# A planner that knows how TensorE's array is divided: biases planned head by head, and times nearer to the trace

## The chip, the cores and the metric

The kernel runs on one core of a Trainium2 chip. The metric is the device time of the whole kernel in microseconds; of the kernel before it is 848.01 us, the median of three runs (847.74 to 849.63). One more execution was profiled: it took 847.26 us, and the rows below are from it.

A core has five engines that run side by side, each through its own list of instructions in order: TensorE (PE, matrix products; PEld is its loading of weights), VectorE (DVE), ScalarE (ACT), GpSimd (POOL) and SyncE (SP, which here issues DMA transfers). They wait for each other by semaphores.

## What is computed

A windowed attention with a few global keys, then two feed-forward networks (FFN), each on the output of the one before. Cut to what matters:

```python
# attention: batch 2, 8 heads, 768 positions, 64 per head
scores = q @ k.T / sqrt(64) - slope[head] * dist       # kept: 96 positions back, 8 global keys
a = exp(scores - max); a = a / (a.sum() + 1e-9)
x = (a @ v) as 1536 tokens x 512

# first FFN: 4 experts, all applied, weighted by p of the token; 512 -> 1024 -> 512
out = sum over e of p[:, e] * (relu(x @ w1[e]) @ w2[e])

# second FFN: 512 -> 2048 -> 512; w_in and w_out arrive as 64-bit floats
h = out @ w_in;  g = h * clip(h + 3, 0, 6) / 6;  return g @ w_out
```

## The kernel before

**Attention.** The work is 24 pairs of a chunk of 256 queries and two heads. For a pair TensorE makes the scores (L351: products with 64 rows, the two heads in the two halves of the array's rows), VectorE adds the bias and takes the smallest value (L366), ScalarE the exponential (L381), VectorE the sums (L392, L393), POOL normalises (L401), TensorE transposes (L420, the whole array), ScalarE and VectorE copy the result out (L437, L442), and TensorE multiplies by the values (L457: 64 columns, the two heads in the two halves of the array's columns).

**FFNs.** Both run as 48 steps: 0 to 31 for the four experts of the two batches, 32 to 39 for the second FFN of batch 0 and 40 to 47 of batch 1. A step forms the first product of two blocks of 128 hidden columns by seven smaller products (m1 to m7, six matmuls of 384 columns each: a high and a low part stand for one fp32 number, L909, L913, L916). m1, m6, m7 and m4 add up in one PSUM bank ("x"), between them ScalarE takes snapshots of it (L933); m2, m5 and m3 go through another bank ("w"), and VectorE adds a snapshot to each of them (L946): m2 makes the corner c11, m5 c22, m3 c12. The bank is free for the next product when the corner is read. The corners become the hidden parts hh and hl (second FFN: L1000, L1003, L1017, L1023), and the second product "O" uses them in 48 matmuls of 512 or 256 columns a step (L1088, L1091, L1092). Weights come in as "wr" (L775), go through ScalarE (the high part, L250) and VectorE (the low part, L255), for steps of batch 0 also through sums (L832).

**Conversions.** The second FFN's weights are 64-bit floats. Beside the steps of the first FFN, 32 conversions turn half a step's weights each into fp32: a load (L691), seven VectorE instructions (L701, L707, L713, L720, L725, L731, L743), and a store to DRAM (L747). Conversions 30 and 31 are the last: the load of step 39's w1 (L775) waits for conversions 28 and 30, that of its w2 for 29 and 31.

**What sets the order.** A planner (class Plan) is given each piece of work with an engine, a cost in us, what it comes after, and a rank. `emit` simulates the engines by these costs: the engine that is free first takes the ready piece of the lowest rank, and the instructions are written out in that order, which each engine then keeps. A piece on another engine is ready LATENCY (0.25 us) after the one that it waits for, after a load 2.0. Where the simulation shows TensorE idle in the attention, small filler matmuls are put in (L263). So the table of costs decides the order on all engines at once. The ranks: a conversion has 100000 and more, behind all else, so it gets VectorE when nothing else is ready. The functions that the diff touches, and what calls them:

Of the kernel before, what the change touches and what calls it, by code (L numbers as in the profile page):

```python
# [17 lines left out]
ALU = mybir.AluOpType  # L18
# [3 lines left out]
P = 128  # L22
# [13 lines left out]
WIN = FAR + P  # L36
# [9 lines left out]
FIRST_LOAD = 1.0  # L46
HUGE = 3.0e38
NEG = -1.0e9
T_SCORES, T_TURN, T_VALUES = (0.95, 1.2), (0.8, 1.05), (0.75, 0.97)
NONE = -4.0e12  # L50
SLOPES = [2.0 ** (-8.0 * (h + 1) / H) for h in range(H)]

# [6 lines left out]
class Plan:  # L59
# [5 lines left out]


    LOAD = 2.0
    LATENCY = 0.25

    def __init__(self, idle=None):  # L70
        self.pieces = []
        self.ported = set()
        self.idle = idle

    def add(self, engine, cost, emit, after=(), rank=0.0, port=False):

        self.pieces.append((engine, cost, emit, after, rank))
        if port or engine == "pool":
            self.ported.add(len(self.pieces) - 1)
        return len(self.pieces) - 1  # L80
# [9 lines left out]
    def emit(self):  # L90
        n = len(self.pieces)
        missing, ready, followers = [0] * n, [0.0] * n, [[] for _ in range(n)]
        free, later, now, ended = {}, {}, {}, {}
        port = 0.0
        for i, (engine, _, _, after, _) in enumerate(self.pieces):
            after = set(self.flat(after))
            missing[i] = len(after)
            for a in after:
                followers[a].append(i)
            free.setdefault(engine, 0.0)  # L100
            later.setdefault(engine, [])
            now.setdefault(engine, [])
        for i in range(n):
            if not missing[i]:
                heappush(later[self.pieces[i][0]], (0.0, i))
        count = 0
        while count < n:
            best = None
            for engine in free:
                while later[engine] and later[engine][0][0] <= free[engine]:  # L110
                    i = heappop(later[engine])[1]
                    insort(now[engine], (self.pieces[i][4], i))

                for place, (rank, i) in enumerate(now[engine]):
                    if i not in self.ported or port <= free[engine]:
                        start = free[engine]
                        break
                else:
                    events = [port] * bool(now[engine]) + [t for t, _ in later[engine][:1]]
                    place, start = None, min(events, default=None)  # L120
                if start is not None and (best is None or start < best[0]):
                    best = (start, engine, place)
            start, engine, place = best
            if place is None:
                free[engine] = start
                continue
            i = now[engine].pop(place)[1]
            count += 1
            _, cost, emit, _, _ = self.pieces[i]
            if i in self.ported:  # L130
                port = start + cost
            if self.idle:
                self.idle(engine, start - ended.get(engine, 0.0))
            emit()
            free[engine] = ended[engine] = start + cost
            for j in followers[i]:
                other = self.pieces[j][0]
                lag = 0.0 if other == engine else self.LOAD if engine == "load" else self.LATENCY
                ready[j] = max(ready[j], start + cost + lag)
                missing[j] -= 1  # L140
                if not missing[j]:
                    heappush(later[other], (ready[j], j))
# [3 lines left out]
def moe_attention_kernel(ctx, tc, qk, vw, sizes, dpt, w1, w2, w_in, w_out, ident_d, fast_d, slow_d, out):  # L146
    nc = tc.nc
# [22 lines left out]
    base = const.tile([P, P + WIN], F32, name="base")  # L170
# [7 lines left out]
    with tc.manual_schedule(engines={mybir.EngineType.DVE}):  # L178
# [3 lines left out]
            out=nv[:, 0:2], in0=nv[:, 2:4], scalar=4294967296.0, in1=lo, op0=ALU.mult, op1=ALU.add  # L182
# [38 lines left out]
    def pools(bx, fast):  # L221
# [43 lines left out]
        plan = Plan(keep_warm)  # L265
# [8 lines left out]
        started = {}  # L274
# [37 lines left out]
        def plan_pair(i, c, hp, tabs, place_users, normalised, biased, outs, x_bank):  # L312
# [40 lines left out]
                            raw[rows, w0 : w0 + WIN][:, used[qb]], start=True, stop=True,  # L353
                        )

            s_in = plan.add("pe", T_SCORES[kinds[0]], scores, [loaded] + waits, rank)
            readers.append(s_in)
            weighed = []
            for qb in range(CH):

                def bias(qb=qb, kind=kinds[qb], used=used[qb]):
                    if "t" not in m:
                        m["t"] = att.tile([P, CH, 2, WIN], F32, tag="t", name=f"t_{u}", bufs=3)
                        m["mn"] = att.tile([P, CH, 2], F32, tag="mn", name=f"mn_{u}", bufs=4)
                    for j in range(2):
                        nc.vector.tensor_tensor_reduce(  # L366
                            out=m["t"][:, qb, j, used], in0=m["s", j][:, qb * WIN : (qb + 1) * WIN][:, used],
                            in1=(base if hp == j == 0 else tabs[:, 2 * hp + j - 1])[:, kind * P : P + kind * WIN],
                            scale=-0.125, scalar=HUGE, op0=ALU.add, op1=ALU.min, accum_out=m["mn"][:, qb, j : j + 1],
                        )  # L370

                after = [s_in, started[2 * hp, kinds[qb]], started[2 * hp + 1, kinds[qb]]]
                e = plan.add("dve", 0.72 if kinds[qb] else 0.5, bias, after + wait_t, rank)
                for su in s_users:
                    su.append(e)
                biased[i].append(e)

                def exponentials(j, qb=qb, used=used[qb]):
                    if "sm" not in m:
                        m["sm"] = att.tile([P, CH, 2], F32, tag="sm", name=f"sm_{u}", bufs=4)  # L380
                    nc.scalar.activation(  # L381
                        m["t"][:, qb, j, used], m["t"][:, qb, j, used], AF.Exp, bias=m["mn"][:, qb, j : j + 1],
                        scale=-1.0, accum_out=m["sm"][:, qb, j : j + 1],
                    )

                for j in range(2):
                    weighed.append(
                        plan.add("act", 0.48 if kinds[qb] else 0.39, lambda j=j, f=exponentials: f(j), [e], rank)
                    )

            def sums():
                nc.vector.tensor_scalar(out=m["sm"][:], in0=m["sm"][:], scalar1=1e-9, scalar2=None, op0=ALU.add)  # L392
                nc.vector.reciprocal(m["sm"][:], m["sm"][:])  # L393

            r = plan.add("dve", 0.4, sums, weighed, rank)
            normal = []
            for qb in range(CH):
                for j in range(2):
# [4 lines left out]
                            scalar2=1.0, op0=ALU.mult, op1=ALU.mult,  # L403
                        )

                    normal.append(plan.add("pool", 0.46 if kinds[qb] else 0.32, normalise, [r], rank))
            normalised[i] += normal
            wait_a, a_users = [], []
            for qb in range(CH):
# [4 lines left out]
            def turn(qb):  # L414
# [7 lines left out]
                            )  # L422

            turns = [
                plan.add("pe", 0.57 if kinds[qb] else 0.3, lambda qb=qb: turn(qb), normal[2*qb:2*qb+2] + wait_a[qb:qb+1], rank)
                for qb in range(CH)
            ]
            t_users += turns
# [30 lines left out]
                                m["at", qb][:n, j, h, :], start=h == 1 - kinds[qb], stop=h == 1,  # L459
                            )  # L460

            v = plan.add("pe", T_VALUES[kinds[0]], values, [e for e, _ in copied] + [v_in, biased[i + 2] if b else outs[i - 2]], rank)
            v_users.append(v)
            for _, at_users in copied:
                at_users.append(v)
# [807 lines left out]
```

## Time and profile before

| | us |
|---|---|
| median of three runs | 848.01 |
| profiled execution | 847.26 |
| its span | 845.2 |
| TensorE busy | 833.7 |
| VectorE busy | 655.2 |
| ScalarE busy | 402.0 |
| POOL busy | 68.1 (all in the attention) |

The span goes from the first instruction to the last; 2.06 us of the execution lie around it. "Busy" counts the time in which an engine works at an instruction; matmuls overlap, so a busy TensorE shows that work is there and not how fast it goes. A wait is listed with the instruction that waited and what ended it last. Starts are counted from the span's start. A row of the timeline gives the start and the busy time; of matmuls the busy time reaches into the next one's, so the time of a matmul among others is read from start to start.

### The profile page before, as it was taken

What the parts mean: (1) busy time and instruction counts of PE and PEld (TensorE: products, weight loads), DVE (VectorE), ACT (ScalarE), POOL (GpSimd) and SP (SyncE); (2) the same over time, 40 slices, a digit from 0 to 9 for tenths busy, and PEclk for the clock granted to TensorE, in tenths of its full rate; (3) what the DMA queues carried; (4) which work ended last, traced back from release to release, by engine and by line L of the source; (5) the groups of instructions that cost most, each with busy time, mean ns of one, the idle gap of its engine ahead of it and who ended that gap; (6) DMA issues with size and microseconds to landing.
All of it is one profiled execution on the core that took longest, in us unless ns stands there. A gap on an engine that the chain in (4) does not pass through costs nothing.

```text
span 845.2 us, 13646 instructions
## 1 busy us (share of the span) xinstructions
PE 833.7 (99%) x5090; PEld 763.2 (90%) x5090; DVE 655.2 (78%) x1366; ACT 402.0 (48%) x850; POOL 68.1 (8%) x131
## 2 busy tenths in 40 slices
PE   8999999999999999999999999999999999999997
PEld 6777999999999999999999999999999999999996
DVE  6999989988998977987777688689898766545442
ACT  6998643543433433543333333335666455545441
POOL 5888200000000000000000000000000000000000
PEclk9999999999999999999999999999999999999999
DMA  7873454465565565645656664744452555534302
GB/s 264 314 221 94 175 202 153 138 211 181 166 209 194 165 222 180 204 150 179 216 172 199 208 208 158 234 165 140 174 163 103 172 186 185 190 125 139 136 1 79
DMA packets 56985, 147.34 MB, mean 174 GB/s; under 512 B 6480, under 2 KB 7760, under 8 KB 56912
## 3 DMA queue, kind: packets, MB, share of 16 engines
q1 hardware_dynamic: 56480, 145.69, 52.2%
q8 instruction: 42, 0.69, 0.3%
q10 hardware_dynamic: 432, 0.71, 0.3%
q14 instruction: 31, 0.25, 0.1%
HBM read 109.66 MB, written 36.72 MB: 173 GB/s over the span
## 4 chain that ended last, share of the span: by engine, by line
PE 92%; DMA 3%; DVE 2%; POOL 1%; ACT 1%; issue 0%; SPq 0%; POOLq 0%; DVEq 0%; ACTq 0%
PE o L1091 16%; PE o L1092 15%; PE o L1088 15%; PE x_x L909 8%; PE x_x L913 8%; PE x_x L916 8%; PE w_w L913 6%; PE w_w L916 6%; PE w_w L909 6%; PE att_q L420 2%; PE att_q L351 1%; PE att_q L457 1%; DMA qkraw<-in_qk 1%; DMA w<-qkraw 1%; POOL t L401 1%; PE att_x L457 1%
## 5 line engine op out<-in xcount | busy, mean ns | idle before, releaser
L1091 PE MATMUL o<-hh,w2l 128*128 128x512 f32 (+1 forms) x768 | 259.4, 338 | 0.0
L1092 PE MATMUL o<-hl,w2h 128*128 128x512 f32 (+1 forms) x768 | 259.0, 337 | 0.0
L1088 PE MATMUL o<-hh,w2h 128*128 128x512 f32 (+1 forms) x768 | 257.8, 336 | 0.0
L933 ACT COPY snap<-x_x 128x384 f32<-128x384 f32 x144 | 68.9, 478 | 195.9 <-PE x_x L916 195.7
L946 DVE TENSOR_TENSOR c_c<-w_w,snap 128x384 f32<-128x384 f32 x144 | 80.0, 556 | 104.4 <-ACT w2h L250 58.5
L1092 PEld LDWEIGHTS o<-hl,w2h 128*128 128x128 f32 x768 | 144.4, 188 | 16.0
L1088 PEld LDWEIGHTS o<-hh,w2h 128*128 128x128 f32 x768 | 144.4, 188 | 13.4
L1091 PEld LDWEIGHTS o<-hh,w2l 128*128 128x128 f32 x768 | 144.5, 188 | 12.7
L909 PE MATMUL x_x<-xoh,w1h 128*128 128x384 f32 x384 | 129.7, 338 | 0.1
L916 PE MATMUL x_x<-xoh,w1l 128*128 128x384 f32 x384 | 129.0, 336 | 0.0
L913 PE MATMUL x_x<-xol,w1h 128*128 128x384 f32 x384 | 128.9, 336 | 0.0
L913 PE MATMUL w_w<-xol,w1h 128*128 128x384 f32 x288 | 97.1, 337 | 0.0
L909 PE MATMUL w_w<-xoh,w1h 128*128 128x384 f32 x288 | 97.0, 337 | 0.0
L916 PE MATMUL w_w<-xoh,w1l 128*128 128x384 f32 x288 | 96.8, 336 | 0.0
L250 ACT CAST w2h<-wr 128x1024 fp32r<-128x1024 f32 x48 | 50.4, 1050 | 61.2 <-PE o L1092 59.1
L909 PEld LDWEIGHTS x_x<-xoh,w1h 128*128 128x128 f32 x384 | 72.3, 188 | 3.2 <-issue 0.6
L913 PEld LDWEIGHTS x_x<-xol,w1h 128*128 128x128 f32 x384 | 72.3, 188 | 2.0
L1015 ACT CAST hh<-c_c 128x384 fp32r<-128x384 f32 x96 | 49.4, 514 | 48.3 <-DVE c_c L984 47.8
L916 PEld LDWEIGHTS x_x<-xoh,w1l 128*128 128x128 f32 x384 | 72.0, 188 | 0.0
L250 ACT CAST w1h<-wr 128x512 fp32r<-128x512 f32 x96 | 46.9, 510 | 49.5 <-PE w_w L913 45.7
L255 DVE TENSOR_TENSOR w2l<-wr,w2h 128x1024 fp32r<-128x1024 f32 x48 | 58.5, 1219 | 2.3 <-ACT w2h L250 2.3
L984 DVE SCALAR_TENSOR_TENSOR c_c<-c_c,p 128x384 f32<-128x384 f32 x96 | 53.8, 561 | 3.2
(90 smaller groups left out, 1132.7 us busy)
## 6 DMA issues: line engine op xcount, KB each, us to landing
wr<-in_w SPq DMA_DIRECT2D x64, 512.0 KB, 3.9
wr<-w SPq DMA_DIRECT2D x32, 512.0 KB, 3.5
kept<-w1h SPq DMA_DIRECT2D x24, 512.0 KB, 3.0
kept<-w1l SPq DMA_DIRECT2D x24, 512.0 KB, 4.8
w1h<-kept SPq DMA_DIRECT2D x24, 512.0 KB, 3.7
w1l<-kept SPq DMA_DIRECT2D x24, 512.0 KB, 4.9
qkraw<-in_w_in SPq DMA_DIRECT2D x16, 512.0 KB, 4.3
w<-qkraw SPq DMA_DIRECT2D x32, 256.0 KB, 4.2
```

Source lines behind the costliest of these rows:

```text
L250: nc.scalar.copy(out_ap, src)
L255: nc.vector.tensor_tensor(out_ap, src, hi_ap.bitcast(F32), op=ALU.subtract)
L909: nc.tensor.matmul(ps_, wh[:, a, cols], xh[:, o, kc, :], start=start and kc == 0, stop=False, skip_group_check=True,)
L913: nc.tensor.matmul(ps_, wh[:, a, cols], xl[:, o, kc, :], start=False, stop=False, skip_group_check=True)
L916: nc.tensor.matmul(ps_, wl[:, a, cols], xh[:, o, kc, :], start=False, stop=last, skip_group_check=True)
L933: nc.scalar.copy(m["n", n][:], m["x"][:, :HT])
L946: nc.vector.tensor_tensor(m[name][:], m["w"][:, :HT], m["n", n][:], op=ALU.add)
L984: nc.vector.scalar_tensor_tensor(out=room_for(), in0=src(), scalar=0.0, in1=p["p"][:, cols], op0=ALU.max, op1=ALU.mult)
L1015: nc.scalar.copy(at(0), room_for())
L1088: nc.tensor.matmul(o, wh, hh, start=first and own and f == 0, stop=False, skip_group_check=True)
L1091: nc.tensor.matmul(o, wl, hh, start=False, stop=False, skip_group_check=True)
L1092: nc.tensor.matmul(o, wh, hl, start=False, stop=end, skip_group_check=True)
```

## The change

The costs of the attention's pieces on TensorE, VectorE and POOL are lowered, and LATENCY goes from 0.25 to 0.12. Pieces of TensorE get a mode: "rows" for scores, "columns" for values, none for transposes and products. TensorE no longer takes the lowest rank alone: among the first 12 ready pieces it takes the one with the lowest rank plus 3.0 where its mode is another than the last piece's, and a change of mode costs 0.1 in the plan. The bias of a pair, one piece for both heads before, is now one piece for each head, and an exponential comes after its own head's bias alone.

```diff
-T_SCORES, T_TURN, T_VALUES = (0.95, 1.2), (0.8, 1.05), (0.75, 0.97)
+T_SCORES, T_TURN, T_VALUES = (0.87, 1.15), (0.22, 0.45), (0.65, 0.86)
+SWITCH, SWITCH_RANK = 0.1, 3.0
...
-    LATENCY = 0.25
+    LATENCY = 0.12
...
+                if engine == "pe" and now[engine]:
+
+                    place = min(
+                        range(min(len(now[engine]), 12)),
+                        key=lambda k: now[engine][k][0] + SWITCH_RANK * (self.modes.get(now[engine][k][1]) != mode),
+                    )
+                    if best is None or free[engine] < best[0]:
+                        best = (free[engine], engine, place)
+                    continue
...
+            if engine == "pe" and self.modes.get(i) != mode:
+                mode = self.modes.get(i)
+                cost += SWITCH
...
-            s_in = plan.add("pe", T_SCORES[kinds[0]], scores, [loaded] + waits, rank)
+            s_in = plan.add("pe", T_SCORES[kinds[0]], scores, [loaded] + waits, rank, mode="rows")
...
-                e = plan.add("dve", 0.72 if kinds[qb] else 0.5, bias, after + wait_t, rank)
...
+                for j in range(2):
+                    after = [s_in, started[2 * hp + j, kinds[qb]]]
+                    e = plan.add(
+                        "dve", 0.32 if kinds[qb] else 0.21, lambda j=j, f=bias: f(j), after + wait_t, rank
+                    )
...
-                        plan.add("act", 0.48 if kinds[qb] else 0.39, lambda j=j, f=exponentials: f(j), [e], rank)
+                        plan.add("act", 0.48 if kinds[qb] else 0.39, lambda j=j, f=exponentials: f(j), [shifted[j]], rank)
...
-            r = plan.add("dve", 0.4, sums, weighed, rank)
+            r = plan.add("dve", 0.36, sums, weighed, rank)
...
-                    normal.append(plan.add("pool", 0.46 if kinds[qb] else 0.32, normalise, [r], rank))
+                    normal.append(plan.add("pool", 0.44 if kinds[qb] else 0.32, normalise, [r], rank))
...
-                plan.add("pe", 0.57 if kinds[qb] else 0.3, lambda qb=qb: turn(qb), normal[2*qb:2*qb+2] + wait_a[qb:qb+1], rank)
+                plan.add("pe", T_TURN[kinds[qb]], lambda qb=qb: turn(qb), normal[2*qb:2*qb+2] + wait_a[qb:qb+1], rank)
```

The values' piece gets mode="columns" in the same way. The instructions are the same in both kernels, but for seven fillers fewer; what differs is their order. The lines of the new kernel have numbers higher by 18 to 21 (L351 is now L369, L743 is L764). Three places show it; a row is line, operation, output<-inputs and size, and the number behind the first letters of a tile is the step.

First, TensorE at the start of the attention, around the third scores (att_q0); L263 and L281 are fillers, L420 and L441 transposes. Before:

```order
L263 MATMUL w_ps_139<-idle_85 128x192
L351 MATMUL att_q0_210<-qkraw_62 128x232
L351 MATMUL att_q1_211<-qkraw_62 128x232
L351 MATMUL att_q0_210<-qkraw_62 128x232
L351 MATMUL att_q1_211<-qkraw_62 128x232
L420 MATMUL att_q4_282<-qkraw_62,t_0_0_221 128x128 x2
L420 MATMUL att_q5_292<-qkraw_62,t_0_0_221 128x128 x4
L351 MATMUL att_q2_250<-qkraw_62 128x128
```

Now:

```order
L369 MATMUL att_q3_255<-qkraw_62 128x232
L441 MATMUL att_q4_264<-qkraw_62,t_0_0_217 128x128 x2
L369 MATMUL att_q0_210<-qkraw_62 128x232
L369 MATMUL att_q1_211<-qkraw_62 128x232
L369 MATMUL att_q0_210<-qkraw_62 128x232
L369 MATMUL att_q1_211<-qkraw_62 128x232
L441 MATMUL att_q5_291<-qkraw_62,t_0_0_217 128x128 x4
L369 MATMUL att_q2_254<-qkraw_62 128x128
```

The first two transposes stood behind the third scores, and now stand ahead of them.

Second, VectorE around the last instruction of conversion 31 (L743, now L764, which writes qkraw alone), with the corners of step 39 (c_39_c11, L946, now L967) and low parts of weights (w1l, w2l, L255, now L273). Before:

```order
L1003 SCALAR_TENSOR_TENSOR qkraw_62<-qkraw_62,c_38_c12_7192 128x384
L255 TENSOR_TENSOR w1l_40_7184<-wr1_40_7163,w1h_40_7183 128x256
L743 TENSOR_TENSOR qkraw_62<-qkraw_62 128x512
L1023 SCALAR_TENSOR_TENSOR hl_38_7131<-qkraw_62,hh_38_7130 128x384
L946 TENSOR_TENSOR c_39_c11_7253<-w_39_w_7235,snap_39_1_7242 128x384
L1003 SCALAR_TENSOR_TENSOR qkraw_62<-qkraw_62,c_39_c11_7253 128x384
L1023 SCALAR_TENSOR_TENSOR hl_39_7274<-qkraw_62,hh_39_7273 128x384
L946 TENSOR_TENSOR c_39_c22_7299<-w_39_w_7266,snap_39_3_7291 128x384
L1003 SCALAR_TENSOR_TENSOR qkraw_62<-qkraw_62,c_39_c22_7299 128x384
```

Now:

```order
L752 SCALAR_TENSOR_TENSOR qkraw_62<-qkraw_62 128x512
L967 TENSOR_TENSOR c_39_c11_7248<-w_39_w_7231,snap_39_1_7239 128x384
L273 TENSOR_TENSOR w1l_39_7198<-wsum_39_7206,w1h_39_7197 128x1024
L1024 SCALAR_TENSOR_TENSOR qkraw_62<-qkraw_62,c_39_c11_7248 128x384
L764 TENSOR_TENSOR qkraw_62<-qkraw_62 128x512
L273 TENSOR_TENSOR w1l_40_7184<-wr1_40_7228,w1h_40_7183 128x512
L1044 SCALAR_TENSOR_TENSOR hl_39_7270<-qkraw_62,hh_39_7269 128x384
L273 TENSOR_TENSOR w1l_40_7184<-wr1_40_7228,w1h_40_7183 128x256
L967 TENSOR_TENSOR c_39_c22_7316<-w_39_w_7282,snap_39_3_7306 128x384
```

The conversion's last instruction stood ahead of the corner c11 of step 39. Now it stands behind that corner, the low part of 1024 columns and one piece of the activation (L1024).

Third, TensorE ahead of step 39's first product (x_39). Before:

```order
L1092 MATMUL o_32_3_6447<-hl_37_6978,w2h_37_6943 128x512
L1088 MATMUL o_32_3_6447<-hh_37_6977,w2h_37_6943 128x512
L1091 MATMUL o_32_3_6447<-hh_37_6977,w2l_37_6955 128x512
L1092 MATMUL o_32_3_6447<-hl_37_6978,w2h_37_6943 128x512
L909 MATMUL x_39_x_7217<-xoh_0_137,w1h_39_7105 128x384
L913 MATMUL x_39_x_7217<-xol_0_138,w1h_39_7105 128x384
```

Now:

```order
L1109 MATMUL o_32_4_6353<-hh_38_7099,w2h_38_7068 128x256
L1112 MATMUL o_32_4_6353<-hh_38_7099,w2l_38_7079 128x256
L1113 MATMUL o_32_4_6353<-hl_38_7100,w2h_38_7068 128x256
L1109 MATMUL o_32_4_6353<-hh_38_7099,w2h_38_7068 128x256
L1112 MATMUL o_32_4_6353<-hh_38_7099,w2l_38_7079 128x256
L1113 MATMUL o_32_4_6353<-hl_38_7100,w2h_38_7068 128x256
L930 MATMUL x_39_x_7219<-xoh_0_137,w1h_39_7197 128x384
L934 MATMUL x_39_x_7219<-xol_0_138,w1h_39_7197 128x384
```

The O matmuls just ahead of it belonged to step 37's hidden parts (hh_37). Now 12 of 256 columns and 6 of 512 more stand ahead of it, the last of them with step 38's (hh_38).

## Rows read from the trace of the kernel before

**Rows 1.** The page: busy us of each engine, share of the span, instructions.
```profile
PE 833.7 (99%) x5090; PEld 763.2 (90%) x5090; DVE 655.2 (78%) x1366; ACT 402.0 (48%) x850; POOL 68.1 (8%) x131
```

**Rows 2.** What TensorE waited for: us in total, times, longest us.
```profile
PE att_q L420 <- DVE at L437: 1.2, 1, 1.2
PE att_q L351 <- DMA qkraw<-in_qk: 1.1, 2, 0.7
PE att_x L457 <- DVE at L437: 0.5, 1, 0.5
```

**Rows 3.** The chain that ended last, 676 to 706: start, us, what.
```profile
687.70 0.61 DVE qkraw L743
688.33 5.50 DMA w<-qkraw
693.90 4.63 DMA wr<-w
698.55 1.06 ACT w2h L250
...
702.31 0.44 PE x_x L909
```

**Rows 4.** Timeline of TensorE, 687 to 706: start, busy us, instruction.
```profile
687.46 0.39 PE L1092 MATMUL o<-hl,w2h 128*128 128x512 f32 x1
687.68 0.33 PE L909 MATMUL x_x<-xoh,w1h 128*128 128x384 f32 x1
...
701.78 0.28 PE L1091 MATMUL o<-hh,w2l 128*128 128x256 f32 x1
701.90 0.28 PE L1092 MATMUL o<-hl,w2h 128*128 128x256 f32 x1
...
705.55 0.34 PE L909 MATMUL w_w<-xoh,w1h 128*128 128x384 f32 x1
```

**Rows 5.** Timeline of TensorE in the attention, 46 to 50.
```profile
46.08 1.09 PE L420 MATMUL att_q<-qkraw,t 128*128 128x128 f32 x8
47.10 0.89 PE L351 MATMUL att_q<-qkraw 64*128 64x128 f32 x8
...
49.40 0.66 PE L420 MATMUL att_q<-qkraw,t 128*128 128x128 f32 x4
49.89 0.58 PE L263 MATMUL w_ps<-idle 128*128 128x192 bf16 x5
```

**Rows 6.** Timeline of TensorE at the start, 8.6 to 12; idle before in brackets.
```profile
8.60 1.05 PE L351 MATMUL att_q<-qkraw 64*128 64x232 f32 x8
10.12 1.66 PE L420 MATMUL att_q<-qkraw,t 128*128 128x128 f32 x6 [0.46 <-POOL t L401]
11.70 0.89 PE L351 MATMUL att_q<-qkraw 64*128 64x128 f32 x8
```

**Rows 7.** The page's costliest groups: xcount, busy us, mean ns, idle before.
```profile
L933 ACT COPY snap<-x_x 128x384 f32<-128x384 f32 x144 | 68.9, 478 | 195.9 <-PE x_x L916 195.7
...
L255 DVE TENSOR_TENSOR w2l<-wr,w2h 128x1024 fp32r<-128x1024 f32 x48 | 58.5, 1219 | 2.3 <-ACT w2h L250 2.3
```

**Rows 8.** Timeline of one step of the first FFN, all engines, 202 to 204.
```profile
202.96 0.33 PE L909 MATMUL x_x<-xoh,w1h 128*128 128x384 f32 x1
...
203.22 0.56 DVE L946 TENSOR_TENSOR c_c<-w_w,snap 128x384 f32<-128x384 f32 x1 [0.40 <-ACT w2h L250]
...
204.00 0.39 PE L1088 MATMUL o<-hh,w2h 128*128 128x512 f32 x1
```

**Rows 9.** Timeline of SyncE's DMA issues, 670 to 677.
```profile
670.18 0.32 SPq L747 DMA_DIRECT2D w<-qkraw  x1
672.25 4.83 SPq L775 DMA_DIRECT2D wr<-w  x2
```

**Rows 10.** Timeline of VectorE, 680 to 681.
```profile
680.39 0.55 DVE L946 TENSOR_TENSOR c_c<-w_w,snap 128x384 f32<-128x384 f32 x1
```

**Rows 11.** The page's DMA issues: count, KB each, median us to landing.
```profile
w<-qkraw SPq DMA_DIRECT2D x32, 256.0 KB, 4.2
```

More of the change, by code (lines that the diff above doesn't have):

```diff
@@ L72, in __init__, with add @@
         self.ported = set()
+        self.modes = {}
         self.idle = idle
-    def add(self, engine, cost, emit, after=(), rank=0.0, port=False):
+    def add(self, engine, cost, emit, after=(), rank=0.0, port=False, mode=None):
         self.pieces.append((engine, cost, emit, after, rank))
+        if mode:
+            self.modes[len(self.pieces) - 1] = mode
         if port or engine == "pool":
@@ L94, in emit @@
         port = 0.0
+        mode = None
         for i, (engine, _, _, after, _) in enumerate(self.pieces):
@@ L359, in plan_pair, with bias @@
             for qb in range(CH):
-                def bias(qb=qb, kind=kinds[qb], used=used[qb]):
+                def bias(j, qb=qb, kind=kinds[qb], used=used[qb]):
                     if "t" not in m:
@@ L364, in bias @@
                         m["mn"] = att.tile([P, CH, 2], F32, tag="mn", name=f"mn_{u}", bufs=4)
[L365 to L372, printed above, removed]
-                e = plan.add("dve", 0.72 if kinds[qb] else 0.5, bias, after + wait_t, rank)
-                for su in s_users:
-                    su.append(e)
-                biased[i].append(e)
+                    nc.vector.tensor_tensor_reduce(
+                        out=m["t"][:, qb, j, used], in0=m["s", j][:, qb * WIN : (qb + 1) * WIN][:, used],
+                        in1=(base if hp == j == 0 else tabs[:, 2 * hp + j - 1])[:, kind * P : P + kind * WIN],
+                        scale=-0.125, scalar=HUGE, op0=ALU.add, op1=ALU.min, accum_out=m["mn"][:, qb, j : j + 1],
+                    )
+                shifted = []
+                for j in range(2):
+                    after = [s_in, started[2 * hp + j, kinds[qb]]]
+                    e = plan.add(
+                        "dve", 0.32 if kinds[qb] else 0.21, lambda j=j, f=bias: f(j), after + wait_t, rank
+                    )
+                    s_users[j].append(e)
+                    biased[i].append(e)
+                    shifted.append(e)
                 def exponentials(j, qb=qb, used=used[qb]):
@@ L460, in values @@
                             )
-            v = plan.add("pe", T_VALUES[kinds[0]], values, [e for e, _ in copied] + [v_in, biased[i + 2] if b else outs[i - 2]], rank)
+            v = plan.add("pe", T_VALUES[kinds[0]], values, [e for e, _ in copied] + [v_in, biased[i + 2] if b else outs[i - 2]], rank, mode="columns")
             v_users.append(v)
```

## The prediction

> **What bounds the kernel now.** I read the busy line first [rows 1]: TensorE is busy 833.7 of 845.2 us and VectorE 655.2, so nearly every microsecond of the end is a TensorE microsecond, and a gain must come out of the 11 us in which it isn't busy. The list of TensorE's waits says where [rows 2]: three entries at lines of the attention, 2.8 us together. The FFNs have one stall, which the chain of waits shows [rows 3]: the last conversion of the 64-bit weights (VectorE L743, 687.70), its store, the load back and the cast, then a low part, a corner and two small pieces, and TensorE's next product at 702.31. Without the wait it would start at 702.02 (the matmul ahead of it starts at 701.90, and from one of its kind to the next are 0.12 [rows 4]). So the stall is 0.3 us, and this background chain has no slack left: whatever delays it by one microsecond delays the end by one.
>
> **The sum is made against** the profiled execution, 847.26 us (span 845.2 and 2.06 around it). The median of the runs is 848.01, 0.75 more; what I add goes on the median.
>
> **Part 1, the order in the attention.** The planner now keeps pieces of TensorE together that divide the array alike. What does a switch cost? Eight transposes are busy 1.09 and four 0.66, so 0.11 each. Four take 0.49 from 49.40 to the filler behind them, which divides the array as they do: 0.05 more than 4 x 0.11, the switch at their start. Eight take 1.02 from 46.08 to the scores behind them: 0.14 more than 8 x 0.11, the switches on both sides [rows 5]. Counted in the two orders, the attention has 81 switches before and 77 now, at 0.05 to 0.14: 0.4 us less. Of the fillers 28 stand in it before and 21 now, at 0.58 for five [rows 5]: 0.7 less where TensorE has other work in their place. I take -1.0, with bounds -1.4 and 0.
>
> Against it stands the start (the first order rows ahead). Before, the third scores run from 8.60 while POOL normalises; the first transposes start at 10.12 and six of them hold until 11.70, 1.58 for 0.66 of work, so 0.9 of waiting inside [rows 6]. Now two transposes stand ahead of the third scores. POOL's work is the same, so they can't start before 10.12; the scores follow at 10.4 and last 1.0 (the row's 1.05 less the overlap at its end), the other four transposes run until 12.0, and with two switches what started at 11.70 starts at 12.2: +0.5, bounds 0 and +1.0.
>
> The biases planned head by head let an exponential start after one bias and not after two, and the nearer times change the mix; the waits of 1.2 and 0.5 for VectorE at L437 [rows 2] may shrink or move. I take no net gain: VectorE has the same instructions, and an order that shifts one wait makes another. Bounds -2.8 (all of [rows 2]) and +2.8 (as much again).
>
> At the handover to the FFN, one product fewer stands before the last values (11 and 12), loads for steps 0 to 2 stand later in SP's queue, and VectorE has eight pieces ahead of step 1's first corner, among them two low parts of 1.22 [rows 7], about 5.8 us in one line. TensorE has no wait there before. I take +0.8, bounds 0 and 1.5. Together the attention and the handover come to -1.0 + 0.5 + 0.8 = +0.3, which I take as zero, with bounds -3 and +4.
>
> **Part 2, the order in the FFNs.** A latency of 0.12 in place of 0.25 lets the planner put second, sixth, fifth and seventh product side by side in some thirty steps, with no O pieces between. The fifth overwrites the bank that the corner c11 reads. In a step of before the second ends and the sixth starts at 202.96, and the corner runs from 203.22 to 203.78; the sixth lasts until 204.00 [rows 8], where now the fifth would follow. That leaves 0.2, under the cover that VectorE is free at that moment, as it was in this step (idle 0.40 ahead of the corner). I take nothing; if VectorE is busy with one more piece of 0.56, the corner is 0.3 late, and in thirty steps that is +9, the upper bound. The TensorE work itself is the same.
>
> **Part 3, the last conversions, the term that decides.** The change doesn't touch them; the order does. On VectorE, conversion 31's last instruction stood ahead of step 39's first corner. Now it stands behind it, and behind a low part of 1024 columns and one more piece (the second order rows ahead). The whole train is one conversion later: conversion 30, which had its store issued at 670.18 [rows 9], now ends behind the corner c22 of step 38. That corner runs at 680.39 for 0.55 [rows 10], and two conversion pieces behind it at 0.61 [rows 3] bring its end to 682.1.
>
> First stall. The store lands 4.2 later (the median of 32 [rows 11]), the load some 4.4 later (a little less than the 4.63 of [rows 3]): 690.7. Two sums (0.3 each) and a low part of 512 columns (0.6), scaled from the 1.22 for 1024 columns [rows 7], bring the third matmul of step 39's first product to 691.9, and so its first, 0.35 ahead, to 691.6. On TensorE that product stood at 687.68. Ahead of it stand now 18 O matmuls that didn't (the third order rows ahead show the last of them): 6 of 512 columns at 0.22 and 12 of 256 at 0.12 [rows 4], so 690.44. Stall 1.2.
>
> Second stall. VectorE has nine pieces from 690.7 on (five of 256 columns at 0.3 and one of 512 at 0.6 by the same scaling, three of the conversion at 0.61 [rows 3]: 3.9), then the corner 0.56 [rows 8], the low part 1.22 [rows 7], a piece of the corner's size and the conversion's last 0.61, less 0.1 where pieces overlap. Conversion 31 ends at 697.4, against 688.3 before. Then its own chain of [rows 3], with the median store in place of its 5.50: 4.2 + 4.63, cast 1.06, low part 1.22, corner c12 0.56 and 0.1 of issue: 709.2. That corner frees the bank for step 40's second product, which stands at 705.55 [rows 4], less the 0.3 stall, less one product of 1.04 [rows 8] that stood ahead of it and now stands behind, plus the first stall: 705.4. Stall 3.8. Two products on the other bank follow side by side, and a snapshot must come between them: 0.48 [rows 7] and the 0.26 from a product's end to its reader [rows 8], 0.75.
>
> Sum 1.2 + 3.8 + 0.75 - 0.3 = +5.45. Nothing hides it: TensorE has no gap from there to the end that could take it up.
> Bounds: stores as quick as conversion 30's (issued 670.18, the load behind it 672.25: 2.1 [rows 9]) leave no first stall and 0.8 of the second, so +1.25; stores of 5.50 as the last one [rows 3] make 2.7 + 5.0 + 0.45 = +8.15. I take the median store, since nothing in the profile says which of the two is the rule.
>
> The Trainium skill, "DMA: Bandwidth & Descriptors", section "Anatomy of one DMA", prices a transfer at a fixed 2.0 us and its bytes at 436 GB/s. An estimate by that page is 2.6 for the 256 KB store and 3.2 for the 512 KB load; by it there is no first stall, 0.1 of the second, and the part comes to about +0.5. The rows of this very chain, 5.50 and 4.63 with other transfers in flight, speak against it.
>
> **The rivals.**
> A, quiet transfers: both stores land in some 2.1, the conversions cost +1.25 or less, and the rest cancels: 848.5 to 849.3. For it speaks 670.18 to 672.25 [rows 9]; against it the last store's 5.50, in the very stretch where the conversions now land. 0.17.
> B, faster: the biases by head remove the waits of [rows 2], 2.8, beside switches and fillers 1.0, less 0.5 at the start, so -3.3. It wins only where the conversions cost less than that, so with quick stores again: -3.3 + 1.25 gives 846.0. Stores of 3.1 instead of 2.1, two in a row, turn it around. 0.15.
> C, crowded products: the corner c11 misses its 0.2 in most of the thirty steps, +9 beside +5.45: 862.5. For it speaks how thin that margin is; against it, that VectorE stood idle ahead of the corner [rows 8]. 0.07.
> D, the attention and the handover get worse: VectorE's line ahead of step 1's corner and an order with less room cost the upper bound of +4 beside the conversions' +5.45: 857.5. 0.09.
>
> **How the numbers follow.** The forecast, conversions +5.45 and the rest near 0, has 0.52: 848.01 + 5.4 gives 853.4, by itself 850 to 857. What a measurement of this kernel can't tell from no change is 0.2%, 1.7 us. Faster by more is B, 0.15; within it A, 0.17; slower the forecast, C and D, 0.68. The range for 8 in 10 goes from 846.5 (most of B left out) to 858.5 (D in, C out).
>
> **What would show it.** In the profile after: a wait of TensorE of about 1.2 us near 691 and one of 3.8 near 705; the chain through the conversion's last instruction (at 697 and not 688), the store, the load back, the cast and the corner c12; at the start the third scores behind two transposes; the end of the last values within 1 us of before. The forecast is wrong if TensorE runs without a gap from 680 to 710, if the conversions end as early as before, or if gaps between sixth and fifth product show in most steps.

## The result, and the profile after

The changed kernel takes 853.58 us, the median of eight runs (850.73 to 855.45), and the kernel before 848.25 (847.74 to 849.63, eight runs): 1.0059 times as long, with an interval from 1.0046 to 1.0071. The forecast of 853.4 is met, but by luck: other terms than those that it names make up the sum, and what follows is mostly on that. The profiled execution took 853.45 us with a span of 851.5, 6.3 more than the profiled one of before.

The page's busy line answers to [rows 1]:

```profile
PE 836.0 (98%) x5083; PEld 763.7 (90%) x5083; DVE 651.0 (76%) x1366; ACT 402.7 (47%) x850; POOL 65.8 (8%) x131
```

TensorE is busy 2.3 us longer, over the same matmuls but for seven fillers fewer, and idle 4 us longer. Its waits answer to [rows 2]; in total us, times, longest:

```profile
PE att_q L441 <- POOL t L422: 2.1, 3, 1.3
PE att_q L441 <- DVE sm L413: 1.6, 1, 1.6
...
PE w_w L930 <- DVE c_c L967: 0.9, 1, 0.9
PE x_x L937 <- DVE w1l L273: 0.7, 1, 0.7
...
PE x_x L930 <- ACT snap L954: 0.6, 1, 0.6
PE att_q L369 <- DMA qkraw<-in_qk: 0.4, 1, 0.4
```

The wait of 1.2 for VectorE at L437 and that of 1.1 for a transfer are gone or small (0.4), as rival B hoped. New are 1.6 for VectorE's sums (L413), 1.3 at a time for POOL's normalising, and four smaller ones at the handover and in the FFNs.

**Where the time went.** The FFNs' matmuls are the same in both kernels. I give each its pitch (0.231 us with 512 columns, 0.116 with 256, 0.174 in the products) and compare the moments at which both kernels have done the same sum of them. At 20 us of such work the new kernel is 3.3 behind, at 600, in step 38, 4.0, and at 620, in step 40, 5.8; from there to the end nothing is added. So 3.3 come from the attention and the handover, 0.7 from the steps up to 38, and 1.8 from the late conversions.

**The attention.** The timeline of TensorE, start and busy us, answers to [rows 6]; behind the dots, the second place where it waits:

```profile
7.85 1.05 PE L369 MATMUL att_q<-qkraw 64*128 64x232 f32 x8
10.19 0.68 PE L441 MATMUL att_q<-qkraw,t 128*128 128x128 f32 x2 [1.28 <-POOL t L422]
10.80 1.05 PE L369 MATMUL att_q<-qkraw 64*128 64x232 f32 x8
...
20.39 0.25 PE L281 MATMUL w_ps<-idle 128*128 128x192 bf16 x1
22.21 0.63 PE L441 MATMUL att_q<-qkraw,t 128*128 128x128 f32 x4 [1.58 <-DVE sm L413]
22.77 1.72 PE L478 MATMUL att_x<-at,v 104*64 104x128 f32 x16
```

The start is as forecast: two transposes ahead of the third scores, scores at 10.80, and what stood at 11.70 now runs at 12.4. The wait ahead of the first transposes is 1.28. The wait of 1.58 at 22.21 was not in the forecast. VectorE's timeline shows where it comes from:

```profile
18.51 0.08 DVE L383 DVE_READ_ACCUMULATOR2_ANT mn<- 128x1 f32 x1
19.67 0.17 DVE L599 TENSOR_TENSOR gate_sum<-gate 128x12 f32<-128x12 f32 x1 [1.08 <-DMA gate<-in_dpt]
...
20.86 0.60 DVE L605 TENSOR_TENSOR gate<-gate,gate_sum 128x12 f32<-128x12 f32 x4
21.39 0.68 DVE L458 COPY at<-att_q 128x512 f32<-128x512 f32 x1
21.99 0.15 DVE L413 TENSOR_SCALAR sm<-sm 128x4 f32<-128x4 f32 x1
```

The experts' gate (L599 to L605) is small background work, at the same place of VectorE's list as before. It needs a load of 24 KB, and VectorE stood 1.08 us for it, with the copy at 21.39 and the sums at 21.99 behind it, for which POOL and the transposes wait. SyncE's issues say why the load was late:

```profile
14.49 2.13 SPq L341 DMA_DIRECT2D qkraw<-in_qk  x2
16.67 0.43 SPq L607 DMA_DIRECT2D gate<-in_dpt  x1
```

Before, the load stood one place earlier in SP's queue, and went out at 14.3. Now both loads for later pairs stand ahead of it; the second had to wait for its buffer (1.6 us, until TensorE had read it), and the gate's load went out at 16.67. VectorE's wait for it was 0.4 in the kernel before.

What the wait costs doesn't end with it. The windows of 2 us show start:end, length, busy us (and instructions) of TensorE, its weight loads, VectorE, ScalarE and POOL, then TensorE's granted clock, the DMA share and GB/s:

```profile
22.00:24.00 2.00, 1.79 (x18) 1.65 (x20) 1.97 (x11) 1.05 (x4) 1.47 (x4) 0.77 0.82 267
24.00:26.00 2.00, 2.00 (x16) 1.34 (x14) 1.26 (x10) 1.22 (x4) 1.70 (x4) 0.50 0.07 11
26.00:28.00 2.00, 2.00 (x20) 1.66 (x18) 0.55 (x1) 1.34 (x6) 0.68 (x1) 0.88 0.88 267
```

Behind the 1.58 us the granted clock falls to 0.50, that is from 2.4 to 1.2 GHz, until some 26.5. TensorE is busy through most of it. The clock's share that is missing comes to 0.23 x 2 + 0.5 x 2 + 0.12 x 2 = 1.7 us. That is an upper bound of the loss, since part of the missing time falls into waits. What it costs can be read against e9 (below), in which the gate's load is late too and TensorE takes its 720 attention matmuls in the same order: the wait there is 1.40 us and the clock stays full.

```profile
22.33 0.63 PE L444 MATMUL att_q<-qkraw,t 128*128 128x128 f32 x4 [1.40 <-DVE sm L413]
22.89 1.10 PE L481 MATMUL att_x<-at,v 104*64 104x128 f32 x16
```

The same 16 value matmuls are busy 1.10 us and not 1.72. Matmul by matmul the changed kernel is 0.12 ahead of e9 behind the wait (22.21 and 22.33), and 1.44 behind it by 26.8, where the clock is full again. So the fall costs 1.6 us here. In the profile of the kernel before no window of the attention is below 1.00. The fall, with the longer wait ahead of it, is the largest part of the 3.3.

**The late conversions.** The chain answers to [rows 3], start, us, what:

```profile
699.97 0.61 DVE qkraw L764
700.60 2.22 DMA w<-qkraw
...
702.89 3.76 DMA wr<-w
706.67 1.06 ACT w2h L268
707.75 1.02 DVE w2l L273
...
708.89 0.56 DVE c_c L967
...
709.50 0.44 PE w_w L930
...
711.89 0.49 ACT snap L954
...
712.42 0.45 PE x_x L930
```

The steps are those of the forecast: conversion 31's last instruction behind step 39's c11, the store, the load, the cast, the low part, c12, and step 40's second product, which waited 0.92, and then the snapshot between two products of the other bank, 0.57. (From the last matmul's end as it is modelled; from start to start, beyond the pitch, the two are 1.1 and 0.6.) With the 4.1 that the kernel was behind by then, the conversion's end stood forecast at 701.5, and came at 700.6. What differs are the transfers: store 2.22 and load 3.76 where the sum has 4.2 and 4.63, and 3.89 and 3.66 for conversion 30, so that the first stall was 0.2 and not 1.2. The load's 4.63 was one row; the page of the kernel before has the median of all 32 such loads, beside the store's of [rows 11]:

```profile
wr<-w SPq DMA_DIRECT2D x32, 512.0 KB, 3.5
```

The Trainium skill, "DMA: Bandwidth & Descriptors", section "Anatomy of one DMA — SWDGE (gpsimd) path", gives its fixed time and its rate for transfers that GpSimd issues; these are issued by SyncE. Carried over all the same, store and load are 5.8 together, an estimate. Conversion 31's pair took 5.98, conversion 30's 7.55 and that of [rows 3] 10.13: the estimate is nearer than the prediction's rows for the first of the three alone.

### The profile page after: what moved, and what is told of

Read it like the earlier page. It is cut to its first block, busy times and chain, and to the rows that moved or that the text cites. A ratio compares the mean times of both kernels' runs of the same rounds, so it can differ in the third digit from the quotient of the medians.

```text
span 851.5 us, 13646 instructions
## 1 busy us (share of the span) xinstructions
PE 836.0 (98%) x5083; PEld 763.7 (90%) x5083; DVE 651.0 (76%) x1366; ACT 402.7 (47%) x850; POOL 65.8 (8%) x131
## 4 chain that ended last, share of the span: by engine, by line
PE 87%; DVE 5%; DMA 4%; ACT 2%; issue 1%; SPq 0%; POOL 0%; ACTq 0%; POOLq 0%
PE o L1113 15%; PE o L1112 15%; PE o L1109 15%; PE x_x L934 7%; PE x_x L930 7%; PE x_x L937 7%; PE w_w L930 6%; PE w_w L934 6%; PE w_w L937 6%; PE att_q L441 2%; DMA wr<-in_w 1%; PE att_x L478 1%; PE att_q L369 1%; DVE t L383 1%; DMA wr<-w 1%
## 5 line engine op out<-in xcount | busy, mean ns | idle before, releaser
L967 DVE TENSOR_TENSOR c_c<-w_w,snap 128x384 f32<-128x384 f32 x144 | 80.0, 556 | 115.5 <-ACT w2h L268 91.4
L273 DVE TENSOR_TENSOR w2l<-wr,w2h 128x1024 fp32r<-128x1024 f32 x48 | 58.7, 1222 | 2.8 <-ACT w2h L268 2.8
L930 PEld LDWEIGHTS w_w<-xoh,w1h 128*128 128x128 f32 x288 | 54.0, 188 | 3.4 <-DVE c_c L967 2.2
```

The lines of the kernel that those rows point to most:

```text
L273: nc.vector.tensor_tensor(out_ap, src, hi_ap.bitcast(F32), op=ALU.subtract)
L930: nc.tensor.matmul(ps_, wh[:, a, cols], xh[:, o, kc, :], start=start and kc == 0, stop=False, skip_group_check=True,)
L967: nc.vector.tensor_tensor(m[name][:], m["w"][:, :HT], m["n", n][:], op=ALU.add)
```

## The experiments

They ran in three groups (e1 to e4, e5 to e8, e9 to e12), each on one chip with runs of the kernel before, whose medians are 848.45, 848.55 and 849.65; ratios are to these, with their interval. The changed kernel stands at 1.0059 [1.0046, 1.0071].

**e1: the gate's load early.**

```diff
-            a = plan.add("load", 0.2, lambda: nc.sync.dma_start(g[:], dpt.rearrange("e (p n) -> p e n", p=P)), (), 9)
+            early["gate"] = lambda: nc.sync.dma_start(g[:], dpt.rearrange("e (p n) -> p e n", p=P))
...
+            a = plan.add("load", 0.2, lambda: None, (), 9)
...
                 nc.sync.dma_start(m["v"][:], vw[c, hp])
+                if i == 1:
+                    early["gate"]()
```

> The changed kernel, with one DMA moved: the load of the experts' gate (24 KB) is issued behind the second pair's values at the start and not behind two loads of later pairs. The order on TensorE, VectorE, ScalarE and POOL is the same. Theory: VectorE's wait for that load (1.1 us at 18.6) stops TensorE for 1.6 us at 20.6, and behind that wait its clock runs at half for some 3.7 us; without the wait both go, so -3.3 us against the changed kernel, about 850.3, granted clock 1.00 from 20 to 28. Rival (the new mix of the attention costs that much in many places, the wait for the gate only hides another): within 0.7 us of the changed kernel, and the clock falls elsewhere. A middle: -1.6, if the clock falls anyway.

Measured: 853.24 us, 1.0057 [1.0043, 1.0071], no gain. VectorE's wait for the gate is gone, but TensorE's timeline and the windows of this run show the clock falling at another place:

```profile
7.30 1.05 PE L372 MATMUL att_q<-qkraw 64*128 64x232 f32 x8
10.09 0.68 PE L444 MATMUL att_q<-qkraw,t 128*128 128x128 f32 x2 [1.73 <-POOL t L425]
10.69 1.90 PE L372 MATMUL att_q<-qkraw 64*128 64x232 f32 x8
```

```profile
12.00:14.00 2.00, 2.00 (x12) 1.15 (x10) 1.05 (x5) 2.00 (x10) 0.48 (x2) 0.50 0.01 4
```

In this execution the hole at the start, ahead of the first transposes, was 1.73 us and not 1.28, and the clock fell behind it. The hole ends as before, when POOL is done (10.09, and 10.19 in the changed kernel); the scores ahead of it started earlier (7.30 and not 7.85). The rival's words hold: the clock falls elsewhere. So there are two holes, and closing one alone says little on either.

**e2: four conversions ahead; e3: with the gate's load early too.**

```diff
-                rank = 1e5 + n
+                rank = 150.0 + n if n >= 28 else 1e5 + n
```

> The changed kernel, with the last four conversions (28 to 31) planned ahead of the weights' parts (rank 150 and not 100000): conversion 31 ends by step 36's corner c12 instead of behind step 39's c11. Nothing ahead of step 34 moves. Theory: the stalls at 708.6 (0.9) and 711.9 (0.6) are the late conversion, so they go: -1.8 us, about 851.8. Rival (the stalls come from the order of TensorE there, second product straight after third, and not from the conversion): same as the changed kernel within 0.5. The forecast's size (+5.45 from slow stores) would give -5 on average over executions.

> Both edits together. Theory: they are 700 us apart and add up, -5.1 us, about 848.5, no slower than the kernel before. Rival: one hides part of the other, or the attention's new order costs beside them: 850 or more.

Measured: 857.25, 1.0104 [1.0088, 1.0119], and 857.44, 1.0101 [1.0087, 1.0116]: both slower, against either theory. In e2 the stalls at the late conversion are gone (from 600 to 620 us of FFN work it falls behind by nothing more, the changed kernel by 1.8), but TensorE waits earlier, in step 36's neighbourhood:

```profile
677.77 0.44 PE L930 MATMUL x_x<-xoh,w1h 128*128 128x384 f32 x1 [1.67 <-ACT snap L954]
...
681.40 0.44 PE L930 MATMUL w_w<-xoh,w1h 128*128 128x384 f32 x1 [0.96 <-DVE c_c L967]
```

Between 560 and 600 us of work it loses 5.0. The chain behind the first of these waits starts on VectorE: a low part (669.78, 1.23) stood behind the conversions, and the buffer of the next load came free behind it. The load (671.07, 5.20) landed late, and its cast on ScalarE (676.30, 1.04) stood ahead of the snapshot. In e3's profile the same wait is 1.76, and the clock falls behind it as well. This was a bad edit for the question; e6 asks it again.

**e4: LATENCY back at 0.25.**

```diff
-    LATENCY = 0.12
+    LATENCY = 0.25
```

> The changed kernel with LATENCY back at 0.25; mode rule, biases by head and costs stay. With it all conversions stand where they stood before, and the products of a step are no longer side by side; the gate's load is issued one load earlier than in the changed kernel. Theory (the change of LATENCY alone moves the conversions and the products): stalls in the FFNs go, -2.5 us from that; the gate's wait of VectorE shrinks and with it the stall at 20: another -2 to -3; so 848 to 849.5. Rival (the mode rule or the biases by head cost in the attention): -2.5 only, 851.

Measured: 850.48, 1.0026 [1.0017, 1.0035]: between the two. The conversions stand where they stood in the kernel before, and from 20 us of FFN work to the end this run loses nothing against it. The 4.3 that it is behind at 20 are from the attention, where the clock fell behind a wait of 1.56 us at the start, and a wait of 1.28 for VectorE's sums came at 23.16. So 0.12 in place of 0.25 is what moved the conversions.

**e5: fillers in the hole at the start, on e1.** Fifteen small matmuls ahead of pair 0's first transposes:

```diff
             def turn(qb):
+                if i == qb == 0:
+                    for _ in range(15):
+                        nc.tensor.matmul(spare_bank[0][:, 0:192], idle[:, 0:P], idle[:], start=True, stop=True)
```

> The kernel of e1 (the gate's load early), and 15 filler matmuls on TensorE ahead of pair 0's first transposes, in the hole that the two transposes ahead of the third scores leave. They end no earlier than the hole. Theory: in e1 TensorE waited 1.73 us there and its clock then ran at 1.2 GHz from about 10.5 to 14; the fillers take the wait away, so the clock stays at full speed, and the rest of the hole stays: -1.8 us against e1, about 851.4, and without the gate's wait the clock is full all through the attention. Rival (the clock's fall costs nothing, as the engines that TensorE waits for set the time): the clock stays full and the time stays at 853.2.

Measured: 852.23, 1.0045 [1.0031, 1.0059]. No window of the attention is below 1.00, and the last matmul of the values starts at 95.56 and not 97.33: 1.8 earlier, the theory's figure. Matmul by matmul, 1.2 of it are there by 16 us; 0.5 is a wait at 33 that e1 has and this execution hasn't. The median moves by 1.0 only. In this profiled execution the late conversion cost 2.8, in the changed kernel's 1.8 and in e1's 1.3, so its size too is one execution's.

**e6: the last two conversions ahead.** The edit of e2 with 30 in place of 28.

> The changed kernel with the ranks of the last two conversions alone lowered (30 and 31, rank 150): on VectorE they end at c11 and c12 of step 38, and no other piece moves by more than these two. Theory: the late conversion is worth the 1.9 us that the profiled execution of the changed kernel lost between 705 and 713: -1.9, about 851.7. In e2 four conversions went ahead of low parts of steps 36 and 37, whose lateness stopped TensorE at 677 and 681 (2.6 us); two should leave these alone. Rival: whatever is put ahead on VectorE there makes another piece late, so 853.5 or more.

Measured: 851.79, 1.0044 [1.0028, 1.0059]; the profiled execution has no stall left between 600 and 620 us of work. So the profile bears the theory's 1.9 out; in the median it is 1.3 by the ratios, and the intervals overlap.

**e7: LATENCY 0.25 behind the attention alone.**

```diff
                 atx.close()
+                plan.LATENCY = 0.25
```

> The changed kernel with LATENCY at 0.12 until the attention is planned and at 0.25 behind it. The attention's order stays; the order in the FFNs is the old one, conversions too. Theory: all that the changed kernel lost behind 107 us (2.6 in its profile: 0.7 in steps with products side by side, 1.9 at the late conversion) goes: about 851, still slower than before by the attention's 2 to 3.3. Rival: the FFN's order matters little in most executions, and the attention makes the whole difference: 853.

Measured: 852.10, 1.0035 [1.0023, 1.0046]. The median lies between theory and rival. In the FFNs it is as theory says: from 20 us of work to the end the profiled execution gains 0.4 on the kernel before (its one stall of 0.3 is gone). In the attention this execution had both holes, 1.77 and 1.87 us, and the clock fell behind each:

```profile
12.00:14.00 2.00, 2.00 (x12) 1.23 (x10) 1.13 (x5) 2.00 (x10) 0.59 (x2) 0.50 0.00 0
...
26.00:28.00 2.00, 2.00 (x16) 1.65 (x16) 0.88 (x8) 1.44 (x4) 1.97 (x3) 0.50 0.60 149
```

**e8: all three, the fillers, the gate's load and LATENCY 0.25 behind the attention.**

> Fillers in the hole, the gate's load early, and LATENCY 0.25 behind the attention. Theory (the loss is the clock's fall, the gate's wait and the FFN's order, and these add up): about 848.0 to 848.8, the same as before; what is left of the change, the fewer switches, is worth less than 1 us. Rival (the mode rule or the biases by head cost beside these): 850.

Measured: 848.87, 1.0002 [0.9993, 1.0011]: the same as the kernel before, as theory says: with the three taken away, the change is worth nothing that these runs can tell. The same windows and the two places of TensorE's timeline:

```profile
12.00:14.00 2.00, 2.00 (x24) 1.37 (x23) 1.97 (x12) 2.00 (x10) 0.83 (x3) 1.00 0.03 9
...
26.00:28.00 2.00, 2.00 (x26) 1.54 (x23) 1.78 (x11) 1.96 (x8) 1.74 (x4) 1.00 0.81 299
```

```profile
8.22 1.41 PE L441 MATMUL w_ps<-idle 128*128 128x192 bf16 x15
10.01 0.68 PE L447 MATMUL att_q<-qkraw,t 128*128 128x128 f32 x2 [0.38 <-POOL t L425]
...
21.19 0.63 PE L447 MATMUL att_q<-qkraw,t 128*128 128x128 f32 x4 [0.74 <-DVE at L464]
```

The waits are 0.38 and 0.74, and the clock stays full. At 20 us of FFN work this execution is 0.85 behind the kernel before; TensorE still waits at the handover (0.7 for a low part of w1, 0.3 and 0.2 for parts of x, 1.2 together), for which the forecast has +0.8. What the fewer switches and fillers give back against it isn't separated.

**e9 and e10: one of the two alone.** e8 without the gate's early load, and e8 without the fillers.

> e8 without the gate's early load: the fillers fill the first hole, and LATENCY is 0.25 behind the attention. Theory: VectorE's wait for the gate stops TensorE for some 1.6 us near 20.5, and its clock then falls once: 848.9 + 0.9 (the longer wait) + 1.7 (the clock) = 851.5. Rival (the first hole alone matters): 849.

> e8 without the fillers: the gate's load is early, the first hole stays at some 1.7 us. Theory: the clock falls once, behind the first hole: 848.9 + 1.7 = 850.6, and no fall near 22. With e7 (852.1, neither), e9 and e8 (848.9, both) this makes a square; if the two holes add up, e9 + e10 - e8 is e7 + 0.5 or nearer.

Measured: 849.75, 1.0008 [0.9998, 1.0018], and 850.01, 1.0003 [0.9991, 1.0016]. Both come out nearer to e8 than theory has it, and the two don't add up to e7. In e9 the hole at 20.9 was 1.40 us and the clock did not fall behind it; in e10's profiled execution it was 1.71 at the start, the clock fell there and the last matmul of the values starts 1.85 later than in e8; 0.45 of that is there at the first scores already, whose load came later. The last one of e9 starts 1.95 later than in e8 without a fall: 0.47 at the first scores, 0.7 at the longer wait, and 0.8 at a wait for a load at 33.4. So a single execution can differ by as much through its loads.

e10's twelve runs go from 848.22 to 852.6, and the mean clock of each run tells them apart. Profiled executions without a fall have 0.998 or 0.999, those with one fall 0.996 or 0.997, those with two 0.994. All of e8's runs have 0.998 or more, and of e9's all but one, which has 0.997. Of e10's, six have 0.997 or less, with a median of 850.7, and six more, with one of 849.5. So e10's hole makes the clock fall in about half of its executions, and there it costs some 1.3 us; e9's late load seldom or never makes it fall. The intervals can't tell e9 and e10 from e8, so that e8 needs both edits is not shown.

**e11: e8 without the mode rule.**

```diff
-SWITCH, SWITCH_RANK = 0.1, 3.0
+SWITCH, SWITCH_RANK = 0.0, 0.0
```

> e8 with the mode rule taken out (SWITCH and SWITCH_RANK 0): 84 changes of mode in the order and not 78. The theory of the prediction, 0.05 to 0.14 us a change: +0.3 to +0.8, so 849.2 to 849.7. Rival (the rule costs more by delaying pieces of low rank than it saves): 848.5 or less.

Measured: 858.53, 1.0108 [1.0089, 1.0126]: worse than either theory has it. In e8 the FFN's first product starts at 55.95, right behind transposes, and the next ones stand between the pairs of the attention. Here the first starts at 73.26; later, ahead of the last pairs, TensorE stands for the split of x. The first row is e8's, the others are e11's:

```profile
55.95 0.42 PE L940 MATMUL x_x<-xoh,w1h 128*128 128x384 f32 x1
```

```profile
73.26 0.42 PE L940 MATMUL x_x<-xoh,w1h 128*128 128x384 f32 x1
...
84.36 0.69 PE L944 MATMUL x_x<-xol,w1h 128*128 128x384 f32 x1 [1.68 <-DVE xol L274]
84.85 0.52 PE L947 MATMUL x_x<-xoh,w1l 128*128 128x384 f32 x1
85.17 0.52 PE L940 MATMUL x_x<-xoh,w1h 128*128 128x384 f32 x1
...
88.88 0.69 PE L940 MATMUL x_x<-xoh,w1h 128*128 128x384 f32 x1 [2.55 <-ACT xoh L269]
```

Each matmul behind 84 takes 0.32 from start to start and not 0.17: the clock is at 1.2 GHz there as well. Products and transposes have no mode, so behind transposes the rule prefers a product to scores of lower rank by less than 3.0. It draws products forward, between the pairs; that is worth far more here than the six changes of mode. This holds with the new costs: the kernel before has no such rule, and starts its first product at 53.48.

**e12: the biases of a pair as one piece again,** with the gate's load early and LATENCY 0.25 behind the attention.

> The gate's load early, LATENCY 0.25 behind the attention, and the biases of a pair as one piece again (0.64 and 0.42 in the plan); no fillers added, since the planner itself puts the third scores ahead of the first transposes again and two fillers before them. Theory: the first hole comes from the biases planned head by head, which let transposes be planned early; without them no hole, no fall of the clock, and 848.0 to 848.9. Rival (the hole comes from the lower costs): the clock falls at 10 again, 850.5.

Measured: 850.92, 1.0020 [1.0010, 1.0030]. The third scores do stand ahead of the first transposes again, with two fillers before them, and TensorE has no wait there:

```profile
11.19 1.05 PE L372 MATMUL att_q<-qkraw 64*128 64x232 f32 x8
12.18 0.88 PE L441 MATMUL att_q<-qkraw,t 128*128 128x128 f32 x6
...
86.00:88.00 2.00, 2.00 (x9) 1.90 (x9) 0.00 (x0) 0.71 (x2) 2.00 (x6) 0.50 0.36 137
```

The clock stays full at the start (the last row is a window). The lower costs are still in, so the hole comes from the biases planned head by head. But the clock falls near 86, behind waits of 0.53, 0.82 and 1.05 us for the copies of VectorE and ScalarE, and all twelve runs have a mean clock of 0.997 or less. The time is near the rival's figure, for another reason than the rival's.

## Why the prediction was right, and where it was not

- The direction and the size of the whole were right (+5.3 measured, +5.4 forecast). Two terms were not, and their errors cancel: +5.45 for the late conversions was 1.8 in the profile, and 0 for the attention and the handover was 3.3. That the sum came out is luck.
- Part 3, the late conversions: the mechanism was right step by step, the chain, the bank and the snapshot. The size was not: +5.45 forecast, 1.8 measured. The term that failed is the transfers, "the median store" of 4.2 and the load of 4.63; they took 2.22 and 3.76. The sum took a median for the store and a single slow row for the load, whose median on the same page is 3.5; with 3.5 for both loads the sum's own steps give about +3.4. The rest is the last store, quick as in rival A, while conversion 30's took 3.89 and not A's 2.1. The quick bound, +1.25, was nearer than the forecast. e6 and e7 show that the stall is this chain's.
- Part 1, taken as zero: +3.3 in the profile. The start held (+0.5 forecast, +0.7 measured). At the handover (+0.8 forecast) the waits come to 1.2, with a low part of w1 the longest; e8, where the rest is taken away, is 0.85 behind. The -1.0 for switches and fillers shows nowhere by itself. The sign that the last values end within 1 us of before failed: their last matmul starts at 97.96, and before at 95.66. What failed is the step "I take no net gain" for the waits in the middle: VectorE's list was weighed by its pieces' durations, and the wait for the gate's load inside it was left out. The load had been moved past one wait for a buffer in SP's queue, the kind of move that the handover's term counts and this one doesn't.
- What the forecast has no term for is the clock. A hole was priced at its length; where the clock falls behind it, it costs its length and another 1.3 to 1.6 us. The upper bound of +4 holds the part all the same.
- Part 2, products side by side: 0.7 in the whole, from a few steps. The cover failed in another way than the forecast says, VectorE being busy with one more piece: in the step at 207 it stood for a load ahead of the corner, in its order.

```profile
206.64 0.43 DVE L853 TENSOR_TENSOR wsum<-wr 128x256 f32<-128x256 f32 x1 [1.27 <-DMA wr<-in_w]
206.98 0.55 DVE L967 TENSOR_TENSOR c_c<-w_w,snap 128x384 f32<-128x384 f32 x1
...
207.58 0.19 PEld L930 LDWEIGHTS w_w<-xoh,w1h 128*128 128x128 f32 x1 [0.40 <-DVE c_c L967]
```

The fifth product's weight load waited 0.40 for the corner, and its first matmul started 0.25 late. Of rival C's +9 little came.
- Of the 2.8 us of waits that rival B counted, 0.4 is left in the same place, and longer ones came elsewhere. D has the nearest mechanism for the attention's part, an order with less room.

## What to carry to other kernels

A wait that stands in an engine's list for a small background transfer belongs to everything behind it; when a planner's times change, look first at what each such transfer now stands behind in its queue. Price a hole on TensorE by what it does to the clock as well as by its length. And take the price of a transfer from all of its rows, store and load alike: here one store took from 2.2 to 5.5 us, so that a slow and a quick case are better kept apart than replaced by one figure.

## What the runs showed of the hardware that was not expected

- TensorE's granted clock went from 2.4 to 1.2 GHz for some 3.5 us, while it had work, behind waits of 1.58 (changed kernel), 1.73 (e1), 2.31 (e2), 1.75 and 1.76 (e3), 1.56 (e4), 1.65 (e6), 1.77 and 1.87 (e7) and 1.71 us (e10), and in e12 behind one of 0.82 and one of 1.05 us close together; in e11 it was down for some 10 us. It did not fall behind 1.22 (kernel before), 1.28 (changed kernel and e4), 1.34 (e2), 1.14 (e6) and 1.40 us (e9) in the attention, nor behind 1.67 (e2) and 1.59 us (e5) in the FFNs. So the length of a wait alone doesn't decide it: 1.67 in e2 and 1.76 in e3 are at the same place, and it fell behind the second only. What else decides is not shown.
- Matmul by matmul, against executions with the same order and a full clock, such a fall cost 1.3 us at the start of the attention (e1, e7 and e10) and 1.5 to 1.6 behind the wait at 20 to 24 (changed kernel, e6 and e7).
- The same hole at the start was 1.14 (e6) to 1.77 us (e7) long in executions of kernels with one order there. It ends at 10.1 to 10.5 in each, when POOL is done; the scores ahead of it end sooner or later. The runs' mean clock follows the time: of the changed kernel's eight, 850.73 us has 0.999 and 855.42 and 855.45 have 0.995. The 4.7 us between them are more than the falls alone.
- The store of 256 KB that a conversion ends with took 2.22, 3.89 and 5.50 us in the three places shown.
